# Attention into two expert layers: the preparation steps of each pair of heads placed one by one, up to two pairs ahead

## The chip, the cores and the metric

The kernel runs on one core of one Trainium2 chip. The metric is the device time of one execution in microseconds (us), lower is better; the median of several runs is given. Engines: TensorE (PE, with its weight loads PEld), VectorE (DVE), ScalarE (ACT), GpSimd (POOL) and SyncE (SP), which here only issues DMAs.

## The reference

Sixteen heads (2 batches of 8) of 576 positions and 64 dimensions go through attention with rotary embedding; its output, 1152 tokens of 512 values, goes through a dense layer and then through four experts, all in float32.

```python
def _attn_ref(q, k, v):
    ...
    q_rot, k_rot = (rotate(q), rotate(k))
    scores = 1.0 / np.sqrt(D) * np.matmul(q_rot, k_rot.transpose(0, 1, 3, 2))
    attn = np.exp(scores - np.max(scores, axis=-1, keepdims=True))
    attn = attn / (np.sum(attn, axis=-1, keepdims=True) + 1e-09)
    return np.matmul(attn, v)
...
h = x @ w_in
x = (h * (1.0 / (1.0 + np.exp(-h)))) @ w_out
for e in range(4):
    out += p[:, e:e + 1] * (np.maximum(x @ w1[e], 0.0) @ w2[e])
```

## The kernel before, in words

**Stages.** `attention` (from L925) handles eight pairs of heads, about 200 us of the span; `moe` (L837) does the dense layer and the experts. Matrix products in attention are accurate to float32: an operand is split into a high and a low part of type float32r, and the products of the parts are added up in PSUM.

**A pair.** For each pair `load1` (L233) loads `xk` and `xq` (128 rows, 2 x 576 values: the heads and, for the sine term, the heads with their halves exchanged; two buffers each). `rotary` (L245) makes three steps of each, called 1, 2 and 3: times cosine, times sine, add. Step 4 rounds to the high part (`key_high` on ScalarE, L257, with the factor 0.125; `query_high`, L271, on GpSimd) and step 5 subtracts for the low part (`key_low` on VectorE, L260; `query_low`, L277, on GpSimd) and spreads the parts. The spread is by DMA, from SBUF to SBUF: `key_spread` (L264, four DMAs of 288 KB into `kk`) and `query_spread` (L280, four DMAs of 144 KB into `qq`), all on SyncE's queue. `kk` and `qq` have two buffers, one for even pairs and one for odd ones. `scores` (L312) then multiplies `qq` with `kk`.

**Units.** A pair has nine units (a block of queries of one head, the ninth for the rest of both heads). The loop at L1035 runs over 72 units; in round i (s = i mod 9 within the pair) it goes through a row of ORDER (ORDER0 in pair 0, ORDER2 in the last two pairs), twelve letters: S scores of unit i+2, M their row maximum (`rowmax`, DVE, L357), E exponential of unit i+1 (`expo`, ACT, L367), T transposes of unit i (PE, L288), H and L their copies from PSUM on ACT (L405) or, for the units in EVD, on DVE (L411), B the row of PLAN (products with `xv`, L441 and L444, and the normalization, L478 to L492), v and V what these leave for ACT and DVE, W and w steps that widen the first dense weights (`widen0`, L94). Only the order on each engine follows from this; semaphores do the rest.

**Placement of the preparation.** The row of GPL, worked through behind the letters, says which rotary and query steps go to GpSimd in that round: lower case names are of the pair after next, K1 to Q3 (in GPL0) and q4, q5 of the next pair. The key's steps 4 and 5 come through `Nk` in PLAN: `key_parts` (L290) at letter B of s = 0, so that the rounding and `key_low` run at letters v and V of s = 1; behind the spread of keys `key_parts` issues the load of `xk` for the pair after, and behind the spread of queries q5 issues that of `xq` (L1029). Scores of the next pair's first unit are taken at s = 7.

**The start.** Pair 0 is prepared in pieces in the order of START (L34): the loads go out in pieces of columns over the queues of SyncE and ScalarE (L943 to L953), rows 0 to 63 (TOP) first. The first five units (NUN) don't wait for the spread: `first_scores` (L341) multiplies the unspread parts `q2` and `k2`, four float32r products for each half of the keys.

Of the kernel before, what the change touches and what calls it, by code (L numbers as in the profile page):

```python
# [14 lines left out]
PLAN = [['Nk', 'L0'], [], ['L1'], ['Ln'], [], ['P0'], [], ['P1'], ['Pn']]
PLAN0 = [[], ['Nk'], [], [], [], ['P0'], ['P1'], [], ['Pn']]
PLAN2 = [['L0', 'Nk'], [], ['L1'], ['Ln'], [], ['P0'], [], ['P1'], ['Pn']]
ORDER = ['ESMTHvwVBWLX', 'SEWvMBXVTHwL', 'ESMTvXHVBwLW', 'BSvTWwEHVXML', 'TVHXESMWwBLv', 'SEwTvMVBXHWL', 'wSVBEvMWTHLX', 'TWEvHSwMLVXB', 'SvETwMHXBLWV']
ORDER0 = ['TXSMEHvVWwLB', 'XEVSwTMHvBLW', 'STBwEvWHMLXV', 'XvSTHMWBLVwE', 'THvVBXWSwMEL', 'TEVSvBwMHXLW', 'vLWSETHwMBXV', 'SETHvVMLwXWB', 'SMXBWTHwLvVE']
# [21 lines left out]
def f32(ap):  # L41
    return ap.bitcast(F32)
# [3 lines left out]
def fused_kernel(ctx, tc, q, k, v, w_in, w_out, dprobs, w1, w2, cst, out):  # L46
# [166 lines left out]
    for p in range(NPAIR):  # L213
        P = Pair()
        P.b, P.hp = divmod(p, H // 2)
        P.n, P.i = p, p % 2
        P.halves = [[0, 1], [2, 3, 4]]
        P.off = {0: 0, 1: 128, 2: 0, 3: 128, 4: 256}
        if P.b == 0:
            P.cols = [[(0, 256, 0)], [(0, 320, 256)]]  # L220
        else:
            P.cols = [[(0, 256, 640)], [(0, 256, 896), (256, 64, 576)]]
        P.W = [sum(64 if r == 4 else 128 for r in h) for h in P.halves]
        P.units = []
# [64 lines left out]

    def key_parts(P):  # L290
        assert (P, "k3") in made
        parts(P, "k")

        def low():
            key_low(P)
            key_spread(P)
            if P.n + 2 < NPAIR:
                load1(pairs[P.n + 2], "k", k)

        evacs.append(lambda: (lambda: key_high(P), low))  # L300
# [624 lines left out]
    def attention():  # L925
# [5 lines left out]
        CA, CB, QA, QB = slice(0, 288), slice(288, 576), slice(0, 256), slice(256, 576)  # L931
# [50 lines left out]
        def eng(name):  # L982
# [13 lines left out]
            "d": all_of(rotary(P0, "q", g, LOW, QA)), "dh": lambda: query_high(P0, g, LOW, QA),  # L996
            "dl": lambda: query_low(P0, g, LOW, QA),
            "e": all_of(rotary(P0, "q", g, ALL, QB)), "eh": lambda: query_high(P0, g, ALL, QB),
            "el": lambda: query_low(P0, g, ALL, QB),
# [7 lines left out]
        }  # L1007
        for name in START:
            steps[name]()
        load1(pairs[2], "k", k)  # L1010
        load1(pairs[2], "q", q)

        def pool_items(N, NN, N3):
            its = {}
            for Z, names in ((N, "KQ"), (NN, "kq")):
                for nm in names:
                    for i in range(3):
                        if Z:
                            its[nm + str(i + 1)] = lambda nm=nm, i=i, Z=Z: rotary(
                                Z, nm.lower(), nc.vector if nm + str(i + 1) in DV1 + DVR else g)[i]()  # L1020
            for Z, nm in ((N, "K3"), (NN, "k3")):
                if Z:
                    its[nm] = mark((Z, "k3"), its[nm])

            def low():
                query_low(N, g)
                query_spread(N)
                if N3:
                    load1(N3, "q", q)  # L1029

            its["q4"] = lambda: (parts(N, "q"), query_high(N, g))
            its["q5"] = low
            return its

        for i, (P, un) in enumerate(allu):  # L1035
# [5 lines left out]
            def background():  # L1041
                items = []
                for what in (PLAN0 if p == 0 else PLAN if NN else PLAN2)[s]:
                    if what[0] == "N":
                        if N:
                            key_parts(N)
                    else:
                        Z, hf = (L, 1) if what[0] == "L" else (P, 0)
                        if Z:
                            items += norm(Z, hf) if what[1] == "n" else av(Z, hf, int(what[1]))  # L1050
                run(items)
# [10 lines left out]

            for atom in (ORDER0 if p == 0 else ORDER if NN else ORDER2)[s]:
# [32 lines left out]
            if s == LV and N:  # L1096
                load_v(N)
# [4 lines left out]
            if s == 0 and N:  # L1102
                its = pool_items(N, NN, pairs[p + 3] if p + 3 < NPAIR else None)
            if N:
                for what in (GPL0 if p == 0 else GPL if NN else GPL2)[s]:
                    if what in its:
                        its[what]()
# [135 lines left out]
```

## Time and profile before

| what | us |
|---|---|
| median of 3 runs | 780.25 (776.92 to 782.39) |
| the profiled execution | 784.98 |
| its span in the profile | 783.2 |
| PE busy in the span | 748.5 (96%) |
| DVE, ACT, POOL busy | 480.6, 296.3, 270.0 |

The profile is one execution; its times count from the span's start. Times below are in microseconds, durations of single instructions in the timeline too. A matmul's end is modelled, so a busy PE isn't PE at its peak. The granted clock is a share of TensorE's full 2.4 GHz.

### The profile page before, as it was taken

How to read it: one execution, taken by the hardware profiler on the slowest of the kernel's cores; microseconds unless marked ns; L12 is line 12 of the kernel's file. 1: busy time of each engine (PE TensorE's matmuls, PEld its weight loads, DVE VectorE, ACT ScalarE, POOL GpSimd, SP SyncE). 2: the span in 40 equal slices, each digit the busy share in tenths (PEclk: the TensorE clock that was granted, in tenths of full speed). 3: DMA queues.
4: the chain of work that ended last, by engine and by line, in shares of the span. 5: the costliest groups of instructions: out<-in, count | busy, mean ns of one | idle time of the engine just before them, and what ended most of it. 6: DMA issues, size and time to landing. Idle time of an engine off the chain costs nothing.

```text
span 783.2 us, 11373 instructions
## 1 busy us (share of the span) xinstructions
PE 748.5 (96%) x4418; PEld 675.7 (86%) x4418; DVE 480.6 (61%) x888; ACT 296.3 (38%) x665; POOL 270.0 (34%) x263
## 2 busy tenths in 40 slices
PE   5978778999999999999999999999999999999998
PEld 4765656677899999999999898998989889898997
DVE  5565566676699989797457354544545445454542
ACT  1544446566452534525324132331413224242330
POOL 4745576461100311302540341615235170332600
PEclk7788889899999999999999999999999999999999
DMA  7855675553033313133101030201203011020002
GB/s 206 197 159 150 167 190 128 140 120 137 2 109 108 108 55 108 55 108 108 42 18 50 1 108 1 75 33 36 73 1 108 1 54 55 0 109 0 1 28 95
DMA packets 27575, 63.52 MB, mean 81 GB/s; under 512 B 3584, under 2 KB 5248, under 8 KB 27520
## 3 DMA queue, kind: packets, MB, share of 16 engines
q1 hardware_dynamic: 25552, 61.94, 26.6%
q10 hardware_dynamic: 1968, 0.84, 0.5%
q8 instruction: 35, 0.57, 0.3%
q14 instruction: 20, 0.16, 0.1%
HBM read 46.39 MB, written 2.36 MB: 62 GB/s over the span
## 4 chain that ended last, share of the span: by engine, by line
PE 88%; DMA 5%; POOL 2%; DVE 2%; issue 1%; ACT 1%; SPq 1%; ACTq 0%; POOLq 0%; DVEq 0%
PE m L766 8%; PE m L767 8%; PE m L768 8%; PE m L695 7%; PE m L694 7%; PE m L693 7%; PE m L577 4%; PE m L578 4%; PE m L579 4%; DMA qq<-q 4%; PE m L601 4%; PE m L600 4%; PE m L602 4%; PE b L441 4%; PE s L327 4%; PE b L288 3%
## 5 line engine op out<-in xcount | busy, mean ns | idle before, releaser
L772 DVE SCALAR_TENSOR_TENSOR acc<-m,dp,acc 128x512 f32<-128x512 f32 (+1 forms) x64 | 47.5, 742 | 108.1 <-PE m L768 108.1
L767 PE MATMUL m<-wl,gh 128*128 128x512 f32 (+1 forms) x292 | 113.1, 387 | 0.0
L766 PE MATMUL m<-wh,gh 128*128 128x512 f32 (+1 forms) x292 | 113.0, 387 | 0.0
L768 PE MATMUL m<-wh,gl 128*128 128x512 f32 (+1 forms) x292 | 112.7, 386 | 0.0
L357 DVE TENSOR_REDUCE nm<-s 128x1 f32<-128x576 f32 x72 | 54.0, 749 | 60.8 <-PE s L327 50.0
L714 DVE SCALAR_TENSOR_TENSOR gl<-g,gh 128x288 fp32r<-128x288 f32 x84 | 50.7, 603 | 45.0 <-ACT gh L713 43.2
L676 POOL TENSOR_TENSOR wl<-raw,wh 128x512 fp32r<-128x512 f32 x21 | 27.2, 1299 | 141.8 <-ACT wh L673 141.8
L589 POOL TENSOR_TENSOR gl<-g,gh 128x384 fp32r<-128x384 f32 x24 | 26.9, 1122 | 142.7 <-ACT gh L588 142.6
L327 PE MATMUL s<-kk,qq 128*128 128x288 f32 x236 | 52.0, 349 | 21.9 <-DMA qq<-q 21.3
L367 ACT ACTIVATE p<-s,nm 128x576 f32<-128x576 f32 x72 | 53.5, 744 | 33.3 <-DVE nm L357 25.8
L695 PE MATMUL m<-xh,wl 128*128 128x288 f32 x224 | 66.1, 295 | 0.0
L694 PE MATMUL m<-xl,wh 128*128 128x288 f32 x224 | 66.0, 294 | 0.0
L693 PE MATMUL m<-xh,wh 128*128 128x288 f32 x224 | 65.9, 294 | 0.0
L768 PEld LDWEIGHTS m<-wh,gl 128*128 128x128 f32 x292 | 54.9, 188 | 11.4
L600 PE MATMUL m<-gh,wh 128*128 128x384 f32 x192 | 64.1, 334 | 0.0
L601 PE MATMUL m<-gh,wl 128*128 128x384 f32 x192 | 64.1, 334 | 0.0
L602 PE MATMUL m<-gl,wh 128*128 128x384 f32 x192 | 64.1, 334 | 0.0
L766 PEld LDWEIGHTS m<-wh,gh 128*128 128x128 f32 x292 | 54.8, 188 | 10.5
L767 PEld LDWEIGHTS m<-wl,gh 128*128 128x128 f32 x292 | 54.8, 188 | 10.3
L327 PEld LDWEIGHTS s<-kk,qq 128*128 128x128 f32 x236 | 38.6, 215 | 28.5 <-DMA qq<-q 13.2
L676 POOL TENSOR_TENSOR wl<-cvt,wh 128x512 fp32r<-128x512 f32 x28 | 36.2, 1295 | 69.7 <-ACT wh L673 69.7
L288 PE MATMUL b<-cs,p 128*128 128x128 f32 x320 | 49.3, 289 | 3.3 <-ACT p L367 3.1
(146 smaller groups left out, 1885.6 us busy)
## 6 DMA issues: line engine op xcount, KB each, us to landing
raw<-in_moe_w_dram SPq DMA_DIRECT2D x16, 1024.0 KB, 5.2
kk<-k SPq DMA_DIRECT2D x32, 288.0 KB, 4.4
raw<-in_moe_w_out_dram SPq DMA_DIRECT2D x8, 1024.0 KB, 4.8
raw<-in_moe_w_in_dram SPq DMA_DIRECT2D x6, 1024.0 KB, 5.0
qq<-q SPq DMA_DIRECT2D x30, 144.0 KB, 6.1
xk<-in_k_dram SPq DMA_DIRECT2D x7, 576.0 KB, 7.4
xq<-in_q_dram SPq DMA_DIRECT2D x7, 576.0 KB, 6.5
xv<-in_v_dram SPq DMA_DIRECT2D x8, 320.0 KB, 6.5
```

The source lines that it names most:

```text
L288: nc.tensor.matmul(o, lhsT, idn[:, 0:n], is_transpose=True, start=True, stop=True)
L327: nc.tensor.matmul(s[:, nb, 0:288], lq, kk[:, a, c:c + 288], start=(a == 0), stop=(a == 1))
L600: nc.tensor.matmul(o, wh[:, f, ds], gh[:, cols], start=(f == 0), stop=False)
L601: nc.tensor.matmul(o, wl[:, f, ds], gh[:, cols], start=False, stop=False)
L602: nc.tensor.matmul(o, wh[:, f, ds], gl[:, cols], start=False, stop=(f == FT - 1))
L676: nc.gpsimd.tensor_tensor(lo, src(name), f32(hi), ALU.subtract)
L693: nc.tensor.matmul(ps, wh[:, k, ms], hh[:, k, cols], start=(first and k == 0), stop=False, skip_group_check=not first)
L694: nc.tensor.matmul(ps, wh[:, k, ms], hl[:, k, cols], start=False, stop=False, skip_group_check=not first)
L695: nc.tensor.matmul(ps, wl[:, k, ms], hh[:, k, cols], start=False, stop=(k == 1), skip_group_check=not first)
L766: nc.tensor.matmul(ps, gh[:, ts], wh[:, f, ds], start=(f == 0), stop=False)
L767: nc.tensor.matmul(ps, gh[:, ts], wl[:, f, ds], start=False, stop=False)
L768: nc.tensor.matmul(ps, gl[:, ts], wh[:, f, ds], start=False, stop=(f == FT - 1))
```

## The change

GPL, `Nk`, `key_parts` and `pool_items` go. Each step of each pair has a place of its own: OFF gives, per step, a slot relative to the pair's first round (round i has slot 2i ahead of its letters and 2i+1 behind them; 18 slots make a pair), OFF1 and OFF2 the places for pairs 1 and 2. So in a steady pair, counted from its start, the slots are: q4 of the next pair 0, `xq` load of the pair after next 1, k5 with the spread of keys (next pair) 2, q5 with the spread of queries (next pair) 4, k1, k2, q2, k3 (after next) 8 to 11, `xk` load (third next) 12, `xv` load (next) 13, q1 16, q3 and k4 (after next) 17. For pair 1, k1, k2, q1, q2 and q3 run on DVE (before, two of the key's steps); later pairs' rotary stays on GpSimd. Loads of pairs 2 on stand at their own slots.

At the start the first loads are whole rows of 576 columns; pair 0's key is scaled in the rotary steps, and `first_scores` multiplies the rotated `xq` and `xk` themselves, one plain float32 product for each half; the parts of pair 0 are made for the spread only. What START leaves over (LATE) goes to slots 0 to 2. The steps d and e (rest of the query) move from GpSimd to DVE. PLAN, ORDER, WIDE, EVD (unit 7's copy from DVE to ACT), RB0 (5 to 6) and DELAY (0 to 4) change too; their rows are left out below, as are the asserts on order.

```diff
-EVD = [1, 3, 8, 4, 7]
-LV = 6
-START = ['ka', 'ah', 'qa', 'd', 'qh', 'al', 'kb', 'bh', 'ql', 'c2', 's0', 'bl', 's1', 'm0', 's2', 'c1', 'dh', 'c3', 'dl', 'm1', 'k0', 'ch', 'e', 'cl', 'x0', 'k1', 'eh', 'el', 'q1', 'q0']
-DV0 = ['c1', 'c2', 'c3']
+OFF = {'k1': -28, 'k2': -27, 'k3': -25, 'k4': -19, 'k5': -16, 'q1': -20, 'q2': -26, 'q3': -19, 'q4': -18, 'q5': -14, 'lk': -42, 'lq': -35, 'lv': -5}
+OFF1 = {'k1': 4, 'k2': 4, 'k3': 6, 'k4': 6, 'k5': 6, 'q1': 0, 'q2': 4, 'q3': 5, 'q4': 6, 'q5': 7, 'lv': 10}
+OFF2 = {'k1': 8, 'k2': 6, 'k3': 14, 'k4': 17, 'k5': 18, 'q1': 9, 'q2': 15, 'q3': 15, 'q4': 19, 'q5': 23, 'lk': 2, 'lq': 5, 'lv': 31}
+DV1 = ['k1', 'k2', 'q1', 'q2', 'q3']
+EVD = [1, 3, 8, 4]
+FIRST = [0, 2, 1, 3, 4, 5, 6, 7, 8]
+START = ['ka', 'kb', 'qa', 's0', 'h', 's1', 'c1', 'c2', 'm0', 'l', 'qb', 'c3', 'ch', 'x0', 's2', 'm1', 'cl']
+LATE = {'d': 0, 'e': 0, 'gh': 1, 'gl': 1, 'k0': 0, 'k1': 0, 'q0': 2, 'q1': 2}
+DV0 = ['c1', 'c2', 'd', 'e']
...
+        def times(z, tab):
+            if P.n == 0 and nm == "k":
+                nc.vector.scalar_tensor_tensor(x[:, z, :], x[:, z, :], 0.125, tab[rows, cols], ALU.mult, ALU.mult)
+            else:
+                g.tensor_tensor(x[:, z, :], x[:, z, :], tab[rows, cols], ALU.mult)
...
         for nb in nbs:
-            for i, (a, z) in enumerate(((0, 0), (0, 1), (1, 0), (1, 1))):
-                c0 = 128 * r + 64 * h
-                nc.tensor.matmul(s[:, nb, 0:288], P.q2[rows, z, c0:c0 + 128],
-                                 P.k2[rows, a, 288 * nb:288 * nb + 288], start=(i == 0), stop=(i == 3))
+            nc.tensor.matmul(s[:, nb, 0:288], P.xq[rows, 0, c0:c0 + 128],
+                             P.xk[rows, 0, 288 * nb:288 * nb + 288], start=True, stop=True)
...
-        load0(nc.sync, P0.xk, k, TOP, CA)
-        table0(TOP, CA)
-        load0(nc.sync, P0.xk, k, TOP, CB)
-        table0(TOP, CB)
-        load0(nc.scalar, P0.xq, q, TOP, QA)
-        load0(nc.sync, P0.xk, k, LOW)
+        load0(nc.sync, P0.xk, k, TOP)
+        table0(TOP)
+        load0(nc.sync, P0.xq, q, TOP)
+        load0(nc.scalar, P0.xk, k, LOW)
+        nc.sync.dma_start(idn, cst[:, 1152:1280])
         table0(LOW)
-        nc.sync.dma_start(idn, cst[:, 1152:1280])
-        load0(nc.sync, P0.xq, q, LOW, QA)
-        load0(nc.sync, P0.xq, q, ALL, QB)
+        load0(nc.sync, P0.xq, q, LOW)
...
+        def prepare(Z):
+            dve = DV1 if Z.n == 1 else DVR
             its = {}
+            for nm, src in (("k", k), ("q", q)):
+                if Z.n > 1:
+                    its["l" + nm] = lambda nm=nm, src=src: load1(Z, nm, src)
+                for j in range(3):
+                    a = nm + str(j + 1)
+                    its[a] = lambda nm=nm, j=j, e=nc.vector if a in dve else g: rotary(Z, nm, e)[j]()
+            its["k4"] = lambda: (parts(Z, "k"), key_high(Z))
+            its["k5"] = lambda: (key_low(Z), key_spread(Z))
+            its["q4"] = lambda: (parts(Z, "q"), query_high(Z, g))
+            its["q5"] = lambda: (query_low(Z, nc.vector if "q5" in dve else g), query_spread(Z))
+            its["lv"] = lambda: load_v(Z)
...
+            for fn in sched[2 * i]:
+                fn()
             for atom in (ORDER0 if p == 0 else ORDER if NN else ORDER2)[s]:
...
+            for fn in sched[2 * i + 1]:
+                fn()
```

## Rows read from the trace of the kernel before

**Rows 1.** The page's 40 slices of 19.6 us: busy tenths, clock and DMA
```profile
PE   5978778999999999999999999999999999999998
...
PEclk7788889899999999999999999999999999999999
DMA  7855675553033313133101030201203011020002
```

**Rows 2.** Waits of PE over the span: total us, times, longest
```profile
PE s L327 <- DMA qq<-q: 21.3, 6, 5.1
```

**Rows 3.** Timeline of PE at pair ends: start, us, what [idle before]
```profile
43.08 1.30 PE L327 MATMUL s<-kk,qq 128*128 128x288 f32 x4 [5.08 <-DMA qq<-q]
...
90.18 1.30 PE L327 MATMUL s<-kk,qq 128*128 128x288 f32 x4 [3.94 <-DMA qq<-q]
...
177.08 0.77 PE L327 MATMUL s<-kk,qq 128*128 128x288 f32 x4 [0.94 <-DMA qq<-q]
```

**Rows 4.** Stretches: length, busy PE, PEld, DVE, ACT, POOL, clock, DMA share, GB/s
```profile
73.00:76.00 3.00, 3.00 (x24) 2.09 (x23) 2.22 (x5) 2.30 (x5) 1.31 (x3) 1.00 0.01 3
...
88.00:91.00 3.00, 0.82 (x3) 0.85 (x4) 0.00 (x0) 0.00 (x0) 2.71 (x2) 0.66 1.02 266
91.00:94.00 3.00, 3.00 (x13) 1.50 (x12) 1.69 (x3) 0.00 (x0) 0.00 (x0) 0.50 0.29 116
```

**Rows 5.** Timeline of PE, L332, each pair's ninth unit (pairs 1, 5, 6, 7)
```profile
59.57 0.79 PE L332 MATMUL s<-kk,qq 128*128 128x288 f32 x4
...
156.25 0.80 PE L332 MATMUL s<-kk,qq 128*128 128x288 f32 x4
174.01 0.77 PE L332 MATMUL s<-kk,qq 128*128 128x288 f32 x4
192.40 0.78 PE L332 MATMUL s<-kk,qq 128*128 128x288 f32 x4
```

**Rows 6.** Timeline of SyncE's queue: issue start, us of issuing, what
```profile
77.46 3.80 SPq L267 DMA_DIRECT2D kk<-k  x4
81.35 1.28 SPq L235 DMA_DIRECT2D xk<-in_k_dram  x1
82.72 3.10 SPq L283 DMA_DIRECT2D qq<-q  x4
...
168.07 3.76 SPq L267 DMA_DIRECT2D kk<-k  x4
```

**Rows 7.** Stretches of stages: columns as in rows 4
```profile
10.00:43.00 33.00, 22.63 (x110) 18.59 (x110) 19.85 (x27) 11.50 (x26) 26.43 (x23) 0.66 0.81 213
...
65.70:90.20 24.50, 20.47 (x129) 15.31 (x129) 15.46 (x28) 12.88 (x30) 14.62 (x14) 0.85 0.61 160
...
158.00:177.00 19.00, 18.13 (x136) 14.01 (x134) 15.46 (x29) 13.01 (x33) 10.85 (x12) 1.00 0.49 116
...
230.00:300.00 70.00, 70.00 (x404) 70.00 (x403) 65.57 (x128) 27.13 (x53) 9.77 (x8) 1.00 0.27 91
```

**Rows 8.** Timeline of the start, DVE, ACT and POOL
```profile
4.69 0.45 DVE L248 TENSOR_TENSOR xk<-xk,cs 64x288 f32<-64x288 f32 x1 [3.65 <-DMA cs<-in_cst_dram]
...
15.08 0.76 DVE L357 TENSOR_REDUCE nm<-s 128x1 f32<-128x576 f32 x1 [0.94 <-PE s L350]
...
19.19 0.74 ACT L367 ACTIVATE p<-s,nm 128x576 f32<-128x576 f32 x1
...
24.23 0.76 DVE L248 TENSOR_TENSOR xk<-xk,cs 128x576 f32<-128x576 f32 x1
24.42 1.83 POOL L250 TENSOR_TENSOR xq<-xq 128x576 f32<-128x576 f32 x1
25.10 1.77 DVE L250 TENSOR_TENSOR xk<-xk 128x576 f32<-128x576 f32 x1
```

**Rows 9.** Timeline of PE: float32r first scores, and float32 products L444
```profile
21.12 4.21 PE L350 MATMUL s<-k,q 64*128 64x288 f32 x16
...
78.00 0.81 PE L444 MATMUL b<-p,xv 128*128 128x320 f32 x2
```

More of the change, by code (lines that the diff above doesn't have):

```diff
@@ L13 @@
 AX = mybir.AxisListType
[L15 to L19, printed above, removed]
@@ L20 @@
-ORDER2 = ['SMXvETHVLBWw', 'TWSvMwBEHVLX', 'vwXSVETWMBHL', 'vBSMTWEVHLXw', 'WwSVTvMEHBLX', 'XVBSvwEWMTHL', 'wVBTEvSXHLMW', 'XTHLSEWMVvwB', 'BEVvSMTWXHLw']
-WIDE = [[6, 10, 11, 13, 15, 17, 18], [18, 22, 23, 25, 28, 30, 32], [30, 35, 36, 39, 40, 43, 46], [42, 46, 47, 49, 51, 53, 54]]
+PLAN = [['L0'], ['L1'], ['Ln'], [], ['P0'], [], [], ['P1', 'Pn'], []]
+PLAN0 = [[], [], [], [], [], ['P0'], ['P1'], ['Pn'], []]
+PLAN2 = [['L0'], [], ['L1', 'Ln'], [], ['P0'], [], [], [], ['P1', 'Pn']]
+ORDER = ['vSEVTwMHXWBL', 'SBTHEwvVXWML', 'SMvXVEwTHWBL', 'vBSWTVEMHXLw', 'STVHMEwBvXWL', 'SVvEwXMWTBHL', 'ETSVwvMHXWLB', 'VTSMvWHEXLBw', 'SWTEHXvMLwBV']
@@ L22 @@
+ORDER0 = ['XETSHvWVMBLw', 'SVETXwMvBWHL', 'TwSvHWEXBVLM', 'SvXMWVTBHLEw', 'TVvHBXWSMwEL', 'vVEXBwSTHLWM', 'EvTHLSWwBVMX', 'VTSEvHMBLWwX', 'WwXSTBHMELvV']
+ORDER2 = ['SvEMXTBHLWVw', 'vWSTMBHLEwXV', 'TvXESwWVMHLB', 'BEvSTVXMHWwL', 'TWVwSMHLEBvX', 'VELXwSBvWTMH', 'TEwBSHXvVMLW', 'TSHLEVMwWvXB', 'vBESMVWTHXwL']
+WIDE = [[6, 10, 12, 14, 16, 17, 19], [18, 22, 24, 26, 28, 29, 32], [32, 35, 37, 39, 42, 44, 46], [42, 46, 48, 50, 51, 52, 55]]
 CONV = [69]
-DELAY = 0
+DELAY = 4
 RB1 = 0
-RB0 = 5
-GPL = [['q4'], ['q5'], [], ['q1', 'k2'], [], ['k1'], ['k3'], ['q2', 'q3'], []]
@@ L229, in fused_kernel @@
         if p == 0:
-            P.units[1], P.units[2] = P.units[2], P.units[1]
+            P.units = [P.units[j] for j in FIRST]
         pairs.append(P)
@@ L246, in rotary @@
         x = getattr(P, "x" + nm)[rows, :, cols]
+        def times(z, tab):
[3 more added lines that the diff above has]
+                g.tensor_tensor(x[:, z, :], x[:, z, :], tab[rows, cols], ALU.mult)
         return [
-            lambda: g.tensor_tensor(x[:, 0, :], x[:, 0, :], CT[rows, cols], ALU.mult),
-            lambda: g.tensor_tensor(x[:, 1, :], x[:, 1, :], ST[rows, cols], ALU.mult),
+            lambda: times(0, CT),
+            lambda: times(1, ST),
             lambda: g.tensor_tensor(x[:, 0, :], x[:, 0, :], x[:, 1, :], ALU.add),
@@ L288, in tr @@
         nc.tensor.matmul(o, lhsT, idn[:, 0:n], is_transpose=True, start=True, stop=True)
[L290 to L300, printed above, removed]
     def prep_small(P):
@@ L346, in first_scores @@
         rows = slice(64 * h, 64 * h + 64)
+        c0 = 128 * r + 64 * h
+        need = {"ka", "kb"} if 1 in nbs else {"ka"}
+        need |= {"e"} if r > 1 else {"c3", "d"} | ({"e"} if r else set()) if h else {"qb" if r else "qa"}
+        need |= {"c3"} if h else set()
+        assert all((P, w) in made for w in need)
         for nb in nbs:
-            for i, (a, z) in enumerate(((0, 0), (0, 1), (1, 0), (1, 1))):
-                c0 = 128 * r + 64 * h
-                nc.tensor.matmul(s[:, nb, 0:288], P.q2[rows, z, c0:c0 + 128],
-                                 P.k2[rows, a, 288 * nb:288 * nb + 288], start=(i == 0), stop=(i == 3))
+            nc.tensor.matmul(s[:, nb, 0:288], P.xq[rows, 0, c0:c0 + 128],
+                             P.xk[rows, 0, 288 * nb:288 * nb + 288], start=True, stop=True)
     def rowmax(P, un):
@@ L930, in attention @@
         TABS = cst[:, 0:1152].rearrange("p (z n) -> p z n", z=2)
-        CA, CB, QA, QB = slice(0, 288), slice(288, 576), slice(0, 256), slice(256, 576)
+        CA, CB = slice(0, 288), slice(288, 576)
+        QA, QB, QC, QD = slice(0, 128), slice(128, 256), slice(256, 576), slice(0, 256)
         P0.xk = yp.tile([128, 2, 576], F32, name="xk")
@@ L995, in attention @@
             "ch": lambda: key_high(P0, LOW), "cl": lambda: key_low(P0, LOW),
[L996 to L999, printed above, removed]
+            "qb": all_of(rotary(P0, "q", eng("qb"), TOP, QB)),
+            "d": all_of(rotary(P0, "q", eng("d"), LOW, QD)),
+            "e": all_of(rotary(P0, "q", eng("e"), ALL, QC)),
+            "gh": lambda: query_high(P0, g), "gl": lambda: query_low(P0, eng("gl")),
             "k0": lambda: key_spread(P0, (0,)), "k1": lambda: key_spread(P0, (1,)),
-            "q0": lambda: query_spread(P0, (0,), QB),
-            "q1": lambda: query_spread(P0, (1,)),
+            "q0": lambda: query_spread(P0, (0,)), "q1": lambda: query_spread(P0, (1,)),
             "s0": lambda: first_scores(*allu[0], (0,)), "s1": lambda: first_scores(*allu[0], (1,)),
@@ L1007, in attention @@
         }
+        steps = {name: mark((P0, name), fn) for name, fn in steps.items()}
         for name in START:
             steps[name]()
-        load1(pairs[2], "k", k)
-        load1(pairs[2], "q", q)
-        def pool_items(N, NN, N3):
+        def prepare(Z):
+            dve = DV1 if Z.n == 1 else DVR
             its = {}
[L1015 to L1033, printed above, removed]
+            for nm, src in (("k", k), ("q", q)):
[9 more added lines that the diff above has]
+            its["lv"] = lambda: load_v(Z)
+            at = {1: OFF1, 2: {a: n - 36 for a, n in OFF2.items()}}.get(Z.n, OFF)
+            for a in ("lk", "lq", "lv", "k1", "k2", "k3", "k4", "k5", "q1", "q2", "q3", "q4", "q5"):
+                if a in its:
+                    n = at[a] if Z.n == 1 else max(0, 18 * Z.n + at[a])
+                    sched[n].append(mark((Z, a), its[a]))
+                    order[Z.n, a] = n
@@ new lines, in attention @@
+        sched, order = {n: [] for n in range(18 * NPAIR)}, {}
+        for name, n in LATE.items():
+            sched[n].append(steps[name])
+        for Z in pairs[1:]:
+            prepare(Z)
+        need = ["lk<k1", "lk<k2", "k1<k3", "k2<k3", "k3<k4", "k4<k5", "lq<q1", "lq<q2", "q1<q3", "q2<q3", "q3<q4", "q4<q5"]
+        for Z in range(1, NPAIR):
+            for w in need:
+                a, b = w.split("<")
+                assert order.get((Z, a), -1) <= order[Z, b]
+            for a, b in (("k5", "k4"), ("q5", "q4")):
+                assert order.get((Z - 1, a), -1) <= order[Z, b]
+            if Z > 2:
+                for a, b in (("k5", "lk"), ("q5", "lq")):
+                    assert order[Z - 2, a] <= order[Z, b]
+            if Z > 1:
+                for a in ("k5", "q5"):
+                    assert order[Z, a] > 18 * Z - 24
+                assert order[Z, "lv"] > 18 * Z - 18 + 2 * max(j for j, x in enumerate(PLAN) if "L1" in x)
@@ L1043, in background @@
                 for what in (PLAN0 if p == 0 else PLAN if NN else PLAN2)[s]:
[L1044 to L1050, printed above, removed]
+                    Z, hf = (L, 1) if what[0] == "L" else (P, 0)
+                    if Z:
+                        items += norm(Z, hf) if what[1] == "n" else av(Z, hf, int(what[1]))
                 run(items)
@@ L1095, in attention @@
                     widening((0, 1, 5))
-            if s == LV and N:
-                load_v(N)
             if s == RB1 and L:
@@ L1101, in attention @@
                 rbc(P, 0)
[L1102 to L1107, printed above, removed]
+            for fn in sched[2 * i + 1]:
+                fn()
             feed.tick(i in CONV)
```

15 lines of the change are left out of this document (5 added, 10 removed).

## The prediction

> **What bounds the kernel now.** I read the 40 slices first [rows 1]. From slice 11 on PE is at nine tenths and more under a full clock, so the two expert stages (about 200 us to the end) are TensorE-bound. The time that can move lies in the first ten, the attention: in the first seven of them PE has digits of 5 to 9, the clock 0.7 to 0.8, and DMA is mostly at 5 to 8 tenths.
>
> Next the waits of PE [rows 2]. One dominates: L327, the scores, waits six times for the DMA that writes `qq`, 21.3 us. The timeline at pair ends gives places [rows 3]: the scores of the next pair's first unit begin at 43.08 and 90.18 after 5.08 and 3.94 us of idleness (three pairs more are like the second), and after only 0.94 us at the last pair (177.08). Four such matmuls took 1.30 us then, 0.77 at the last pair. The stretches show why [rows 4]: in the middle of a pair the clock is 1.00, in the three microseconds around the scores at 90.18 0.66, in the next three 0.50. So a gap is paid twice, as waiting and as a stretch at 1.2 GHz.
>
> The last unit of each pair (L332) marks the pace [rows 5]: 59.57, three pairs more to 156.25, then 174.01, 192.40. The four intervals up to 156.25 sum to 96.68, 24.17 us a pair. Pair 6, without a gap, took 17.76, and pair 7, with the small gap, 18.39.
>
> Why is `qq` late? SyncE's queue [rows 6]: the four `kk` spreads from 77.46 (3.80 us to issue), then the `xk` load of the pair after next (1.28), then four `qq` spreads (3.10), then the `xq` and `xv` loads; the scores begin at 90.18, 12.7 us behind the first `kk`. For pair 7, where no `xk` is left to load, the same chain takes 168.07 to 177.08, 9.0 us. Meanwhile the DMA engines are saturated (share 1.02, 266 GB/s), and nearly idle in the middle of a pair (0.01) [rows 4].
>
> **The change, part by part.**
>
> *Spreads and loads.* k5 (slot -16) puts the low part of the keys and the `kk` spread ahead of the first atom of s=1. Before, key_low came at that unit's V, its eighth atom. A unit is 17.76/9 = 2.0 us, so `kk` starts some 1.5 us earlier in the pair. k4 on ScalarE is already a slot ahead of the pair, so it hides under the previous pair's last exponentials. The `xk` load goes from between `kk` and `qq` to slot 12, the idle middle: that takes 1.3 us out of SP's queue and 0.59 MB out of the burst, 2.4 us at 250 GB/s, a little under the saturated stretch. Against that, the `xq` load (slot 1) now stands directly ahead of `kk`, the same 0.59 MB, though issued some two microseconds sooner. POOL's q5 is at slot 4, half a unit later than before, but `qq` stands behind 3.8 us of `kk` issue anyway.
>
> The balance at an unstalled pace, by [rows 5] and [rows 6]: pair 7's `kk` began 168.07 - 156.25 = 11.8 us behind the previous L332, and a pair takes 17.8; its first score wants to start 2 us behind the L332 of 174.01. That leaves about 8 us for a chain of 9.0 (the 0.94 wait). With 1.5 us gained the wait goes, with half a microsecond to spare; the `xq` load ahead of it may take 0 to 1 us back. Then the full clock stays as well.
>
> *What is late next.* In pairs 1 to 5 POOL works 14.62 us per pair and DVE 15.46; in the stretch of pair 6 POOL had 10.85 of 19.0 and DVE the same 15.46 [rows 7]. So 17.76 carries DVE's load, but not all of POOL's. DMA: share 0.61 x 24.5 = 14.9 us of busy engines per pair, which fits in 18 at 0.82. I take 18.2 per pair: 17.76 plus 0.4 for residual waits. Bounds: 17.0, because PE busy 18.13 of 19.0 us at full clock makes 16.95 of 17.76; 20.5, if 60% of the excess over 18.2 goes. Four pairs: 96.68 - 4 x 18.2 = 23.9 us saved (28.7 to 14.7). Pairs 6 and 7: the 0.94 us gap, 0.9 (0 to 2).
>
> *The start.* Before, the first `xk` rotary begins at 4.69, the first maximum at 15.08 and the first exponential at 19.19 [rows 8]. First loads in whole rows double what must land ahead of the first rotary, to 0.59 MB with the table: 1.2 us later at 250 GB/s, so 5.9; `xq`, 0.3 MB more, by 7.1. Six half-row steps of 0.45 us end at 8.6, and three of the 128-column query, half of that each, at 9.3. Scores need no high and low parts now, so `qh`, `ql`, `ah`, `al` leave the chain. Behind them on DVE stand two LOW steps of 576 columns, 0.76 (24.23) to 1.77 (25.10, beside POOL); at 1.2 the maximum follows at 11.7. c3 on POOL (1.4, bounded by the 1.83 of 24.42) and ch on ScalarE (0.7, as an exponential) end at 13.8, and the first exponential starts there, 5.4 us earlier.
>
> Then DVE gets more: d and e, six steps of some 0.5 us, and for pair 1 five rotary steps where it had two, 0.76 us each: 2.9 + 2.3 = 5.2 us, beside DVE's 13 us of idleness between 10 and 43 (19.85 busy) [rows 7]. Pair 0's `qq` needs e and then POOL's two steps, as before, so I move its issue by a microsecond only; the load of `xk` for pair 2 (slot 2) must wait until PE has read pair 0's `xk` for the fifth unit, and its k2 stands on POOL ahead of pair 1's q5. In bytes, 0.59 MB less precedes pair 1's `qq` (the load for pair 3 goes behind it), 2.4 us. I take 5 us earlier for pair 1's first score (38 instead of 43.08 [rows 3]), between 0 and 8. The gap ahead of it stays.
>
> A row and a rule. DVE's L250 took 1.77 us at 25.10, beside a POOL step from 24.42 that took 1.83; L248 of the same size took 0.76 at 24.23 [rows 8]. The Trainium skill (SBUF — State Buffer, section "Who interferes with whom") says that a VectorE instruction with two SBUF inputs contends with a GpSimd instruction that reads SBUF, and that the second one blocks wholly; this row agrees. By that rule alone every moved DVE step that meets POOL pays 1 us more. That is rival B.
>
> *Plain float32 scores.* Before, two units (16 matmuls) took 4.21 us at the low clock, 2.1 a unit. The nearest float32 matmul, L444, is two records, 0.81 us for 320 columns at the full clock [rows 9]; scaled to 288, the two halves of a unit take 1.46 at the full and 2.9 at the low clock, against 2.1 and half of it. So 0.4 to 0.8 us more on five units, 2 to 4 us of PE, most of it beside DVE-bound waiting; as L350's operands have 64 rows and L444's 128, a gain of 1 us isn't excluded. It is inside the 5 us above.
>
> *Nothing.* DELAY acts on a list that nothing fills. One copy per pair goes from DVE to ScalarE (12.88 busy of 24.5 [rows 7]). RB0, PLAN, ORDER and WIDE move work within a pair without changing it; if their cover is gone, the 0.4 is what I have for it. The expert stage has PE busy throughout (70.00 of 70.00, with DVE at 65.57) [rows 7] and merely starts earlier.
>
> *Sum.* 5 + 23.9 + 0.9 = 29.8. The profiled execution was 784.98 (span 783.2 and 1.8 around it), so 755.2; the median, 780.25, is 4.7 lower: 750.5, in round numbers **750**.
>
> **The rivals.**
> A. *The spread stays late.* The `xq` load ahead of `kk` and the burst of spreads itself keep `qq` behind, so that 60% of the excess goes and the clock still falls: 20.5 a pair, 14.7 + 3 + 0 = 17.7 saved, 762. For it: saturated DMA in the burst [rows 4]. Against: the bytes that left the burst.
> B. *DVE and POOL block each other in pair 0* (the rule above): nine DVE steps more at 1.77 - 0.76 = 1 us each eat the 5, and a second effect in the pairs is small, since DVE's steps there are nearly the same: 24.8 saved, 755. For it: POOL is busy 26.43 of 33 us there [rows 7]; against: DVE's 13 us of idleness.
> C. *The clock does not come up* (the other side). If short waits spread over the pairs in place of one gap, TensorE may stay at 1.2 GHz. Pair 0 shows it: a mean of 0.66 from 10 to 43, with PE busy 22.63 of 33 [rows 7]. 17 us of PE work at full clock would be some 32 (0.77 became 1.30 already where only a part was slow, and the clock halves); four pairs at 32 instead of 24.17 cost 31, less the 5: 806. It decides where over half of a pair's PE work is at the low clock. Against: pair 6 had small waits and kept 1.00.
> D. *The change does not do what it says in the pairs* because a step upstream (POOL in order: k1 to k3, q1 to q3, `rb`, `xl`) sets `qq`: only the start is gained, 775. Against: POOL's 14.62 of 24.5 us leave it room [rows 7].
>
> **How the numbers follow.** Forecast 0.70, A 0.14, B 0.07, C 0.05, D 0.04. The forecast's own bounds are 780 - (8 + 28.7 + 2) = 741.5 and, at 19.2 a pair and 2 at the start, 780 - (2 + 19.9 + 0.5) = 758. With A and B the range is 741 to 766, which leaves out C, D and tails. A measurement here tells about 1%, 8 us, from no change. Faster: forecast, A, B: 0.90 with a tail of A taken off; same: D and that tail, 0.06; slower: C, 0.04.
>
> **What would show it.** Right: L332 intervals of 17 to 19 us from pair 2 on, PE's wait for `qq` below 8 us in all, clock 1.00 behind slice 3, first exponential near 14, `xk` loads issued in the middle of a pair. Wrong: intervals over 20, a wait of scores for `kk` or for ScalarE's exponential in place of `qq`, POOL steps that wait for `xk` or `xq` loads, or a low clock inside the pairs.

## The result: 755.9 us, and the profile after

The changed kernel took 755.87 us (median of 4 runs, 754.77 to 755.96), the kernel before, measured beside it, 781.32 (4 runs, 776.92 to 786.61). The ratio is 0.967 (95% interval 0.961 to 0.973): faster, inside the forecast's range and 6 us above its 750. The profiled execution of the changed kernel took 755.87, with a span of 754.1.

The page's slices after (busy tenths of TensorE, its granted clock, DMA):

```profile
PE   6999999999999999999999999999999999999998
...
PEclk7789999999999999999999999999999999999999
DMA  8877686611233131330110300203012030110002
```

From the second slice on PE is at nine tenths, where [rows 1] had 9 7 8 7 7 8, and the clock is at nine tenths or more from slice 4 on. DMA is busier in most of the first eight slices: about the same bytes (63.7 MB, 63.5 before) flow in less time. The waits of PE (total, times, longest) say why:

```profile
PE s L349 <- DVE xq L258: 3.4, 1, 3.4
PE s L323 <- DMA qq<-q: 3.3, 2, 3.0
```

L323 are the scores that [rows 2] had as L327: 21.3 us of waiting in six waits became 3.3 in two. The timeline shows where these two are, and the pace (L328 is each pair's ninth unit, L332 before; pair 0's came at 34.42 then):

```profile
32.15 0.77 PE L328 MATMUL s<-kk,qq 128*128 128x288 f32 x4
38.90 0.77 PE L323 MATMUL s<-kk,qq 128*128 128x288 f32 x4 [3.04 <-DMA qq<-q]
40.11 1.30 PE L323 MATMUL s<-kk,qq 128*128 128x288 f32 x4 [0.22 <-DMA qq<-q]
...
56.65 0.77 PE L328 MATMUL s<-kk,qq 128*128 128x288 f32 x4
...
94.23 0.76 PE L323 MATMUL s<-kk,qq 128*128 128x288 f32 x4
...
127.79 0.78 PE L328 MATMUL s<-kk,qq 128*128 128x288 f32 x4
...
163.03 0.77 PE L328 MATMUL s<-kk,qq 128*128 128x288 f32 x4
```

Pairs 2 to 5 end at 127.79 - 56.65 = 71.14 us behind pair 1's ninth unit, 17.8 a pair, against 96.68 [rows 5]. Pairs 6 and 7 take 35.24 against 36.15. The score at 94.23 stands where [rows 3] had 90.18, and has no wait. The only gap left is ahead of pair 1 (38.90), and it is still paid twice: the four matmuls at 40.11 take 1.30. The stretches (columns as in [rows 4]) agree:

```profile
42.00:45.00 3.00, 3.00 (x16) 2.35 (x16) 2.87 (x8) 1.02 (x3) 0.00 (x0) 0.50 0.02 7
...
88.00:91.00 3.00, 3.00 (x24) 2.12 (x22) 2.97 (x7) 1.92 (x6) 2.24 (x3) 1.00 1.00 226
91.00:94.00 3.00, 3.00 (x27) 2.87 (x25) 2.12 (x4) 2.23 (x7) 3.00 (x3) 1.00 0.79 211
...
10.00:43.00 33.00, 27.93 (x115) 20.18 (x116) 21.00 (x35) 14.14 (x32) 17.20 (x14) 0.66 0.83 236
```

From 42 to 45 PE is busy throughout and at half clock, while in steady pairs the DMA engines are as saturated as in [rows 4] (share 1.00) and PE works through it at 1.00. In the 33 us from 10 to 43 PE is busy 27.93 instead of 22.63 [rows 7], at the same mean clock. SyncE's queue in a steady pair:

```profile
84.06 3.77 SPq L275 DMA_DIRECT2D kk<-k  x4
87.94 4.43 SPq L291 DMA_DIRECT2D qq<-q  x4
...
93.04 0.45 SPq L236 DMA_DIRECT2D xk<-in_k_dram  x1
```

Nothing stands between `kk` and `qq` now [rows 6] (but once: at pair 2's spreads the `xq` load is issued between them, at 48.26), and `xk` goes out behind `qq`, 7.9 us ahead of the next `kk` (100.91). The start, from the timelines of DVE, PE, ACT and POOL:

```profile
6.12 0.82 DVE L251 SCALAR_TENSOR_TENSOR xk<-xk,cs 64x288 f32<-64x288 f32 x2 [5.08 <-DMA xk<-in_k_dram]
...
9.86 4.21 PE L349 MATMUL s<-xk,xq 64*128 64x288 f32 x8 [3.37 <-DVE xq L258]
12.18 0.76 DVE L356 TENSOR_REDUCE nm<-s 128x1 f32<-128x576 f32 x1 [0.70 <-PE s L349]
...
13.69 0.74 ACT L366 ACTIVATE p<-s,nm 128x576 f32<-128x576 f32 x1
...
24.19 0.75 DVE L253 TENSOR_TENSOR xq<-xq,cs 128x576 f32<-128x576 f32 x1
24.35 1.85 POOL L258 TENSOR_TENSOR xk<-xk 128x576 f32<-128x576 f32 x1 [3.42 <-DVE xk L253]
...
25.99 0.83 DVE L258 TENSOR_TENSOR xq<-xq 128x576 f32<-128x576 f32 x1
```

The first rotary starts later than before (6.12 against 4.69 [rows 8]), the first maximum 2.9 us and the first exponential 5.5 us earlier (15.08 and 19.19 before). The eight float32 records at 9.86 are two units in 4.21 us, to the hundredth what sixteen float32r products took [rows 9].

### The profile page after: what moved, and what is told of

Its sections match the earlier page's. It is cut to its first block, busy times and chain, and to the rows that moved or that the text cites. A ratio compares the mean times of both kernels' runs of the same rounds, so it can differ in the third digit from the quotient of the medians.

```text
span 754.1 us, 11327 instructions
## 1 busy us (share of the span) xinstructions
PE 740.4 (98%) x4398; PEld 667.3 (88%) x4398; DVE 472.5 (63%) x878; ACT 302.5 (40%) x679; POOL 263.4 (35%) x256
## 4 chain that ended last, share of the span: by engine, by line
PE 91%; DMA 3%; DVE 2%; POOL 2%; issue 1%; ACT 0%; POOLq 0%; DVEq 0%
PE m L766 9%; PE m L765 9%; PE m L767 9%; PE m L694 7%; PE m L693 7%; PE m L692 7%; PE m L576 5%; PE m L577 4%; PE m L578 4%; PE m L601 4%; PE m L600 4%; PE m L599 4%; PE b L440 4%; PE s L323 4%; PE b L296 4%; PE m L649 1%
## 5 line engine op out<-in xcount | busy, mean ns | idle before, releaser
L672 ACT CAST wh<-cvt 128x512 fp32r<-128x512 f32 x28 | 17.4, 621 | 89.4 <-DVE cvt L671 89.4
L323 PE MATMUL s<-kk,qq 128*128 128x288 f32 x236 | 48.5, 329 | 3.5 <-DMA qq<-q 3.3
L693 PE MATMUL m<-tf,wh 128*128 128x288 f32 x168 | 49.6, 295 | 0.0
```

The source lines that it names most:

```text
L323: nc.tensor.matmul(s[:, nb, 0:288], lq, kk[:, a, c:c + 288], start=(a == 0), stop=(a == 1))
L693: nc.tensor.matmul(ps, wh[:, k, ms], hl[:, k, cols], start=False, stop=False, skip_group_check=not first)
```

## Experiments

Each ratio is against runs of the kernel before that were measured beside it. Four questions: which edit frees the pairs (e1 to e4), what holds pair 1 (e5 to e7, e9, e10), whether DVE and POOL block each other (e8), what float32 and the whole-row loads do (e11, e12).

**e1: loads back in their old places**, everything else as changed.

```diff
+                    if Z.n > 2 and a in ("lk", "lq"):
+                        n = order[Z.n - 2, {"lk": "k5", "lq": "q5"}[a]]
```

> The changed kernel, but the loads of xk and xq stand where they stood before: xk right behind the kk spread, ahead of the qq spread, xq behind the qq spread. Theory (the SyncE queue and the DMA burst set qq; the load between the spreads costs 1.3 us of issue and 0.59 MB): waits of PE for qq of 1 to 3 us return at the ends of pairs 1 to 4 and the one of pair 0 grows by about 2 us; intervals of pairs 2 to 5 rise from 17.8 to 19.5 to 21.5, total 765 to 772. Rival (the place of k4, k5, q4, q5 alone did it): intervals stay at 17.8, total 756 to 759.

Measured: 767.55 us (765.22 to 770.48), ratio 0.980 (0.975 to 0.985): 11.7 us of the gain gone, as the theory had it. Waits of PE, the queue, and two scores:

```profile
PE s L323 <- DMA qq<-q: 14.9, 5, 5.9
```

```profile
88.45 3.79 SPq L275 DMA_DIRECT2D kk<-k  x4
92.34 1.26 SPq L236 DMA_DIRECT2D xk<-in_k_dram  x1
93.70 3.09 SPq L291 DMA_DIRECT2D qq<-q  x4
...
81.75 0.77 PE L323 MATMUL s<-kk,qq 128*128 128x288 f32 x4 [2.18 <-DMA qq<-q]
...
102.88 1.30 PE L323 MATMUL s<-kk,qq 128*128 128x288 f32 x4 [3.47 <-DMA qq<-q]
```

The order of [rows 6] is back, and the waits with it. The gap of 3.47 us has slow matmuls behind it, that of 2.18 hasn't. Pairs 2 to 5 take 84.0 us, between the 71.1 of the changed kernel and the 96.7 of the kernel before.

**e2: rounding and the spread of keys later** (the spread of queries a slot earlier), loads in their new places.

```diff
-OFF = {... 'k4': -19, 'k5': -16, ... 'q4': -18, 'q5': -14, ...}
+OFF = {... 'k4': -16, 'k5': -15, ... 'q4': -17, 'q5': -15, ...}
```

> The changed kernel, but steps 4 and 5 stand where they stood before (key: behind letters of rounds s = 1, low part and spread at slot -15 instead of -16; query at -17 and -15), loads as in the change. Theory (margin of half a microsecond to two at a pair's end, a slot is one): waits of 0 to 2 us, intervals 17.8 to 19.5 from pair 3 on, total 756 to 764. Rival (the place of the steps is what did it): intervals near 20 or more, total above 766.

Measured: 770.77 us (766.93 to 774.46), ratio 0.985 (0.979 to 0.991), above the theory's range and where the rival put it, though the spread of keys moved by one slot only, about 1 us. DVE, SP and PE in one pair, and two later scores:

```profile
92.86 0.69 DVE L410 COPY pt<-b 128x512 f32<-128x512 f32 x1 [1.64 <-PE b L296]
93.47 0.75 DVE L269 SCALAR_TENSOR_TENSOR k<-xk,k 128x576 fp32r<-128x576 f32 x1
...
94.30 3.78 SPq L275 DMA_DIRECT2D kk<-k  x4
...
104.03 1.30 PE L323 MATMUL s<-kk,qq 128*128 128x288 f32 x4 [2.45 <-DMA qq<-q]
126.31 0.77 PE L323 MATMUL s<-kk,qq 128*128 128x288 f32 x4 [2.35 <-DMA qq<-q]
```

In slot -15 `key_low` (L269) stands on DVE behind that unit's copy (L410), which waits for PE's transposes. So `kk` goes out 94.30 - 80.59 = 13.7 us behind the pair's first score, against 84.06 - 76.21 = 7.9 in the changed kernel; the low clock behind that score (0.50 from 80 to 86) is part of the difference. That isn't the old place either (there `key_low` came ahead of that copy), so e2 shows how sharp the due time is, not what the changed slot is worth.

**e3: both.** The edits of e1 and e2 together.

> Both edits of e1 and e2 together. Theory: the waits add, as all of it is one chain: intervals of pairs 3 to 5 of 21.5 to 24, low clock behind each wait, total 770 to 780. Rival (something else in the change, such as the order of letters or the rotary steps a pair earlier, carries the gain): intervals stay under 19.5, total under 764.

Measured: 774.02 us (773.44 to 774.65), ratio 0.989 (0.985 to 0.993); waits for `qq` 18.3 us in seven. As the theory had it, with e2's reservation.

**e4: the kernel before with the `xk` load moved**, and nothing else.

```diff
             key_spread(P)
-            if P.n + 2 < NPAIR:
-                load1(pairs[P.n + 2], "k", k)
...
             if s == LV and N:
+                if p + 3 < NPAIR:
+                    load1(pairs[p + 3], "k", k)
                 load_v(N)
```

> The kernel before, with one edit: the load of xk for the pair after next leaves its place between the two spreads and goes to the end of round s = 6. Theory: qq lands 2 to 3.7 us earlier (1.3 us of issue, 2.4 us of transfer), the wait of 3.9 us shrinks to 0.5 to 2 and part of the low clock goes with it; intervals of pairs 2 to 5 fall from 24.2 to 19.5 to 22, total 762 to 772. Rival (the spread's start sets it, not the load): total within 3 us of before.

Measured: 756.26 us (755.81 to 757.89), ratio 0.967 (0.963 to 0.971), below the theory's 762 to 772 and level with the whole change. Waits, then the queue, pair 1's ninth unit, a first score and the first exponential:

```profile
PE s L325 <- DMA qq<-q: 3.2, 3, 1.5
```

```profile
66.38 3.77 SPq L267 DMA_DIRECT2D kk<-k  x4
70.25 3.82 SPq L283 DMA_DIRECT2D qq<-q  x4
...
54.48 0.79 PE L330 MATMUL s<-kk,qq 128*128 128x288 f32 x4
...
75.42 0.78 PE L325 MATMUL s<-kk,qq 128*128 128x288 f32 x4
...
19.16 0.74 ACT L365 ACTIVATE p<-s,nm 128x576 f32<-128x576 f32 x1
```

`kk` goes out 11.9 us behind the previous ninth unit (54.48), as it did for pair 7 in the kernel before (11.8), and the score follows 9.0 us later instead of 12.7, without waiting. The ninth units of pairs 1, 5 and 7 are at 54.48, 127.65 and 163.77: pairs 2 to 5 take 73.17 us. One moved load does nearly all that the change does in the pairs; the earlier `kk` and what else changed are worth some 2 us there. From e1, where `kk` is early and the load in the way, the earlier spread, the new start and the rest of the change together are worth 783.39 - 767.55 = 15.8 without the moved load (783.39 is the kernel before, measured beside e1). The two overlap, so they don't add up. The start is as telling: e4 keeps the old one, with the first exponential at 19.16, and yet pair 1's ninth unit comes at 54.48, ahead of the 59.57 of the kernel before and of the 56.65 of the changed one. So the moved load alone brings pair 1 forward, without a new start.

**e5: pair 1 spread head by head.** Its first unit needs head 0 alone.

```diff
-OFF2 = {'k1': 8, 'k2': 6, ...}
+OFF2 = {'k1': 8, 'k2': 7, ...}
...
-            its["k5"] = lambda: (key_low(Z), key_spread(Z))
+            its["k5"] = lambda: (key_low(Z), key_spread(Z, (0,) if Z.n == 1 else (0, 1)))
...
+            its["q5"] = ... if Z.n > 1 else (
+                query_low(Z, g), query_spread(Z, (0,)), key_spread(Z, (1,)), query_spread(Z, (1,)))
```

> The changed kernel, with pair 1's spreads in the order keys of head 0, queries of head 0, keys of head 1, queries of head 1, and the first rotary step of pair 2's keys on GpSimd behind pair 1's query instead of ahead of it. Theory (the wait of 3.0 us for pair 1's first score is the length of the issue chain on SyncE, 7.7 us for eight spreads): the first unit needs four spreads only, so its score begins at 35 to 37 instead of 38.90, the wait falls under 1.5 us, the low clock behind it goes, and the ninth unit of pair 1 comes at 53 to 55 instead of 56.65; total 752 to 754. Rival (the DMA engines are full there: the loads of xk and xq for pair 2, issued at 25.3 and 25.7, go ahead of the spreads): first score at 38 to 39, total 755 to 757.

Measured: 753.93 us (753.79 to 754.64), ratio 0.963 (0.962 to 0.965), as the theory had it. The edit also puts one rotary step of pair 2 (k2) behind pair 1's query; what each half is worth wasn't tested.

```profile
36.03 0.80 PE L323 MATMUL s<-kk,qq 128*128 128x288 f32 x4
...
39.16 0.77 PE L323 MATMUL s<-kk,qq 128*128 128x288 f32 x4 [2.10 <-ACT k L266]
```

The first unit starts 2.9 us earlier and without a wait; the second, of head 1, then waits 2.10. The releaser named, a rounding on ACT, isn't an operand of that score; head 1's `qq` was issued from 34.17 to 35.67, so its transfer is the likelier cause; that isn't shown.

**e6: pair 2's loads and rotary later**, to clear the DMA engines for pair 1's spreads.

```diff
-OFF2 = {'k1': 8, 'k2': 6, 'k3': 14, ... 'q1': 9, 'q2': 15, 'q3': 15, ... 'lk': 2, 'lq': 5, 'lv': 31}
+OFF2 = {'k1': 13, 'k2': 14, 'k3': 15, ... 'q1': 15, 'q2': 16, 'q3': 16, ... 'lk': 7, 'lq': 7, 'lv': 31}
```

> The changed kernel, with the loads of xk and xq for pair 2 behind the spreads of pair 1 on SyncE's queue (slot 7 instead of 2 and 5), and pair 2's rotary steps later on GpSimd (slots 13 to 16). Theory of the full DMA engines: 1.18 MB less ahead of pair 1's spreads, its first score 2 to 4 us earlier than 38.90, wait under 1 us, total 752 to 754, unless pair 2's keys are late then. Theory of the issue chain: the first score stays within 1 us of 38.90, total 755 to 758.

Measured: 756.4 us (755.5 to 757.82), ratio 0.967 (0.964 to 0.969): no gain. POOL's timeline:

```profile
39.69 2.76 POOL L253 TENSOR_TENSOR xk<-xk,cs 128x576 f32<-128x576 f32 x2 [9.81 <-DMA xk<-in_k_dram]
```

Pair 1's first score came 1.3 us earlier (37.57), but POOL lay idle 9.81 us for pair 2's `xk`, and what pair 1 won pair 2 lost. **e7** joins e5 and e6:

> e5 and e6 together. If both the issue chain and the full DMA engines hold pair 1 back, this is the best of the three: first score of pair 1 at 34 to 36 with no wait, total 750 to 753. If one of them alone does, it is as the better of the two.

Measured: 757.32 us (756.39 to 757.69), ratio 0.967 (0.966 to 0.969), worse than e5 alone, by the same late load: POOL is idle for 10.0 us until `xk` is there, the rounding of pair 2's key stands on ACT ahead of an exponential and waits 6.2 us for POOL, and at 45.67 PE waits 3.6 us for that exponential.

**e8: pair 1's rotary on POOL** instead of DVE (`DV1 = []`).

> The changed kernel, with all rotary steps of pair 1 on GpSimd (DV1 empty). Rival B of the prediction (DVE and POOL block each other in pair 0, so the steps on DVE cost as much as they save): total within 2 us of 755.9 or lower. Theory (a step is 0.76 us on DVE and 1.4 on POOL, and pair 1's spreads wait for them): five steps on POOL come to 7 us against 3.8, pair 1's first score 2 to 5 us later than 38.90, total 757 to 761.

Measured: 755.43 us (754.77 to 755.96), ratio 0.965 (0.963 to 0.967): level with the changed kernel. That is the time given to rival B, and the theory's 757 to 761 fell.

```profile
40.28 0.77 PE L323 MATMUL s<-kk,qq 128*128 128x288 f32 x4 [0.86 <-DMA qq<-q]
...
54.99 0.77 PE L328 MATMUL s<-kk,qq 128*128 128x288 f32 x4
```

The first score comes 1.4 us later and the gap is shorter, since pair 0 ends later too (ninth unit 35.70, not 32.15). No slow matmuls follow, and pair 1 takes 19.29 us instead of 24.50; pair 2 is then longer by 1.9. Within these microseconds a pair 0 that ends earlier only waits longer for pair 1's `qq`; e4, whose pair 0 ends at 35.19, agrees. So the total alone doesn't speak for B's mechanism; its rows are read below.

**e9: head by head, and pair 1's units in pair 0's order**, two units of head 0 first (e5 and this edit):

```diff
-        if p == 0:
+        if p < 2:
             P.units = [P.units[j] for j in FIRST]
```

> Pair 1's spreads go head by head (as in the run before that did this) and pair 1's units are also taken in pair 0's order (head 0 of the first two rows, then head 1), so that two units need nothing of head 1. Theory (the second unit waited 2.10 us for head 1's transfer): that wait goes, the first score of pair 1 stays near 36, the clock stays at 1.00, pair 1 takes 19 to 20 us from ninth unit to ninth unit instead of 21.9 and the kernel 751 to 753. Rival (pair 1 is held by DVE and POOL, which prepare pair 2 behind it, and the wait only moves to another unit): pair 1's length stays within 1 us of 21.9 and the time is 753.5 to 756.

Measured: 751.26 us (751.19 to 751.66), ratio 0.960 (0.957 to 0.964). All its runs lie below all of the changed kernel's, so this is the fastest of the versions, as the theory had it.

```profile
39.43 0.77 PE L323 MATMUL s<-kk,qq 128*128 128x288 f32 x4 [1.31 <-DMA qq<-q]
...
51.48 0.77 PE L328 MATMUL s<-kk,qq 128*128 128x288 f32 x4
```

```profile
42.00:45.00 3.00, 3.00 (x20) 1.89 (x20) 0.76 (x1) 2.07 (x6) 2.92 (x5) 1.00 0.98 207
```

The wait is 1.31 us, the clock from 42 to 45 is 1.00 where it was 0.50, and pair 1 takes 51.48 - 32.31 = 19.17 us instead of 24.50. Of these 5.3 us, 4.6 reach the end. So the gap ahead of pair 1, wait and slow stretch together, cost the changed kernel about 5 us; the new order of units is a part of this edit that wasn't tested by itself.

**e10: e9, with pair 1's key added on DVE** (`k3` joins DV1).

> The run before it in this call, and the addition of pair 1's key on DVE instead of POOL. Theory (POOL's chain for pair 1 sets the first score): another 0.5 to 1 us earlier, 750.5 to 752.5. Rival (DVE has no room left in pair 0): its first exponentials come later and the time is 752 to 755.

Measured: 754.74 us (751.73 to 755.23), ratio 0.964 (0.960 to 0.967). Inconclusive. In the profiled execution DVE waited 2.09 us for the table of pair 0's lower rows (0.18 in e9), a load that the edit doesn't touch, and everything behind it was later; what the edit itself costs can't be told from this.

**e11: each float32 product of the first five units twice.**

```diff
         for nb in nbs:
-            nc.tensor.matmul(...)
+            for again in range(2):
+                nc.tensor.matmul(...)
```

> The changed kernel with each of the ten plain float32 products of the first five units issued twice, the second over the first (the output is the same); PE has 20 records of 0.68 us more at the low clock, 13.7 us of busy records or about 10.5 us of time. Theory (the float32 scores stand beside waiting for DVE and ScalarE, and a later start of pair 1 shortens the gap ahead of its first score): a quarter to a half shows, first maximum 2.1 us later, pair 1's ninth unit 2 to 5 us later, 757.5 to 761. Rival (PE sets pair 0, so that float32 counts in full): 764 to 767.

Measured: 765.47 us (764.46 to 766.34), ratio 0.978 (0.975 to 0.982), the rival's 764 to 767. A stretch of PE in pair 0, and pair 0's ninth unit:

```profile
25.00:29.00 4.00, 4.00 (x10) 2.41 (x9) 0.92 (x2) 0.83 (x2) 0.00 (x0) 0.50 0.50 111
```

```profile
40.88 0.78 PE L328 MATMUL s<-kk,qq 128*128 128x288 f32 x4
```

9.6 of the 10.5 us added come through: pair 0's ninth unit is 8.7 later, and PE has no idle time from 25 to 29, at half the clock. The changed kernel itself has PE busy in all of the 12 us from 17 to 29, at 0.50. So from there on pair 0 is bound by TensorE at 1.2 GHz, not by DVE.

**e12: first loads in column pieces again.**

```diff
-        load0(nc.sync, P0.xk, k, TOP)
-        table0(TOP)
-        load0(nc.sync, P0.xq, q, TOP)
+        load0(nc.sync, P0.xk, k, TOP, CA)
+        table0(TOP, CA)
+        load0(nc.sync, P0.xk, k, TOP, CB)
+        table0(TOP, CB)
+        load0(nc.scalar, P0.xq, q, TOP, QD)
...
```

> The changed kernel with its first loads in column pieces again, as in the kernel before. Theory (the pieces cost little, as the first exponential waits for the last of them): first exponential within 1 us of 13.69 and the time within 1.5 us of 755.9. Rival (whole rows are what brings the first exponential from 19.19 to 13.69): first exponential at 15 or later and 757 to 760.

Measured: 754.95 us (754.34 to 756.02), ratio 0.965 (0.961 to 0.969), the same as the changed kernel. The first exponential starts at 14.18, the pair 1 gap is 4.26 us. The theory holds: the whole rows bring nothing that can be measured.

## Why the prediction was right, and where it was not

**Bound and place: right.** The gap ahead of each pair's first score was what could move. e4 shows that the `xk` load between `kk` and `qq` held it: moved alone, it takes the long chain and most of the waits (21.3 us to 3.2) with it.

**Pairs 2 to 5: right within 1.6 us.** Forecast 96.68 - 72.8 = 23.9, measured 96.68 - 71.14 = 25.5; a pair took 17.8, not 18.2. Pairs 6 and 7: 0.9 forecast, 0.9 measured. The `xq` load, feared directly ahead of `kk`, goes out 8.9 us ahead of it (75.15) and took nothing back. The reason was only half right. The forecast gave the wait to an earlier `kk` (1.5 us; measured 11.8 - 9.7 = 2.1, from the ninth unit at 74.33 to 84.06) and gave the load's removal 2.4 us of bytes. The runs show that either helps (e1: 84.0 us for the four pairs; e4: 73.2) and that the load alone is nearly enough: 3.7 us of chain (12.7 to 9.0) against gaps of 3.5 to 5.1 us, whose rest in e4 is 1.5 us or less, with no slow stretch behind it there.

**The start: its own times right, its effect wrong.** Forecast 5, measured 59.57 - 56.65 = 2.9. The first exponential came at 13.69 (forecast 13.8) and pair 1's first score at 38.90 (forecast 38). But pair 0 gained 2.3 us at its ninth unit (34.42 before, 32.15 after), so the gap stayed, and pair 1's first score to ninth unit took 17.75 us where it had taken 16.49. I wrote "The gap ahead of it stays" and still let the first score's gain stand for the end's. And most of the 2.9 is not the start's doing: in e4 the old start with the load moved brings pair 1's ninth unit to 54.48, and in e1 the new start with the load in its old place brings it to 58.36 only, 1.2 us. Of this term the runs bear out the part about bytes ahead of pair 1's `qq`.

**Float32: the term was mis-sized.** Forecast 0.4 to 0.8 us more per unit; measured nothing: 4.21 us for two units before and after, both at the low clock. The 0.81 us of L444 [rows 9] is a duration that overlaps with the next matmul, which starts 0.64 us behind it (78.64); by that pace the same scaling gives 2.3 us a unit at the low clock, near the 2.1 measured. "Most of it beside DVE-bound waiting" was wrong as well: e11 shows that an addition would have counted nearly in full.

**From the profiled execution to the median: the step that missed.** 29.8 us were forecast and 784.98 - 755.87 = 29.1 measured, so the sum itself ended 0.7 us off. That is luck in part: the start was 2.1 us too large and the pairs 1.6 too small. What makes 750 of 755 is the sentence "the median, 780.25, is 4.7 lower: 750.5". It took the profiled run's excess for a constant of that execution. But the kernel before varied by 10 us from run to run (776.71 to 786.61 over all of its runs), and its longer runs had the lower mean clock (786.36 at 0.962, 779.36 at 0.971), whereas the changed kernel's runs lie within 1.2 us. This agrees with an excess that lies in the gaps and slow stretches themselves; then it goes with them, and the sum against the profiled execution, 755.2, was the number to give. That cause rests on this agreement and wasn't tested by itself.

**The rivals.** A (20.5 us a pair) fell: 17.8. C fell: the steady pairs have no wait for `qq` and a clock of 1.00. Its example, pair 0, isn't one of short waits either: its clock is 0.50 while PE is busy throughout (17 to 29 us). D fell: the pairs gained. B named 755, near what came, but not by its mechanism. [rows 8] had DVE at 1.77 beside POOL; after, the DVE step at 24.19 took 0.75 and the one at 25.99 took 0.83 beside a POOL step from 24.35 that took 1.85, where an undisturbed one takes 1.4 (1.41 at 33.41). None of DVE's steps for d, e and pair 1 took more than 0.83, and POOL is busy 17.20 us from 10 to 43 where it was 26.43, so B's price was not paid. e8, which moves pair 1's steps off DVE, ends level, but with a later pair 0. The rule of the Trainium skill (SBUF — State Buffer, "Who interferes with whom") has the instruction that comes second block. That agrees here: DVE came first at 24.19, and POOL, 0.16 us behind it, is the longer one. The rival's mistake was to put the price on all of DVE's nine steps, whoever comes first.

## What to carry to other kernels

Read a serial DMA queue as a chain with a due time: what stands between two transfers that a matmul waits for costs its issue time and its bytes, and moving that one load behind the second of them was worth as much here as the whole rescheduling (756.3 and 755.9 us). Where a gap is also followed by a slow stretch of TensorE, shortening it to the point where the clock holds can pay more than the wait itself. A difference between the profiled run and the median must not be carried over to a kernel that lacks the stalls it may come from; and after a gain at the start, follow it to the next wait before it is counted.

## What was not expected of the hardware

The clock behind gaps. In e2 gaps of 2.60 and 2.45 us ahead of a first score were followed by matmuls of 1.30 us; behind one of 2.35 the score still took 0.77, but the clock was 0.50 from 128 to 130, two microseconds on; behind one of 1.44 it stayed at 1.00. In e1 the gaps of 1.56 and 2.18 had 0.76 and 0.77 behind them and a clock of 1.00, 3.47 had 1.30, but 1.82 had 1.05 and then a clock of 0.50. In e3 the clock stayed at 1.00 behind a gap of 3.13 (84 to 87), and behind one of 3.17 it was 0.50 from 106 to 108. The gap's length alone doesn't decide, and the fall can come a little behind the first score.

The start. From 25 to 29 us in e11 PE was busy 4.00 of 4.00 us, with float32 products from 64 rows and transposes, and its clock was 0.50; a steady pair, as busy, has 1.00. The kernel before, with float32r products there, has the same from 21 to 29 (busy 8.00 of 8.00, clock 0.50), so float32 isn't needed for it. What would raise it there wasn't tried.

Float32 and float32r. One float32 product, two records in the trace, took as long as the four float32r products that it replaced, 1.05 us for 288 columns from 64 rows at the low clock (4.21 for four).
